# Attention scores in quarter-array products inside a fused attention + two-MLP kernel

## The chip, the cores and the metric

One core of one Trainium2 chip runs the whole program. The metric is device time in microseconds (us). The kernel before was run three times: 907.88, 909.35 and 910.19 us, median 909.35.

Engines in the views: PE is TensorE's matmuls, PEld its weight loads (each matmul has one), DVE is VectorE, ACT is ScalarE, POOL is GpSimd, SP issues the DMAs. Each engine runs its own instructions in order.

## The reference

```python
# q, k, v: (4 batches, 8 heads, 576 positions, 64)
scores = q @ k.T / sqrt(64); mask: 0 <= pos_q - pos_k < 64
attn = softmax(scores); x = (attn @ v) -> (2304 tokens, 512)
# first layer:  h = x @ w_in (512 x 2048); g = relu(h)**2; x = g @ w_out
# second layer: h = x @ w_in; g = (a0 + a1 h + a2 h^2 + a3 h^3) / (1 + |b0||h| + |b1|h^2 + 1e-6); out = g @ w_out
```

The weights arrive as float64, everything else as float32.

## The kernel before

**Blocks and layers.** The 2304 tokens are cut into five blocks: four of 512 tokens, one of 256. For each block the first layer runs 16 steps; step `j` makes 128 rows of `h` (line 516: 12 matmuls), squares them on ACT and DVE, and adds their part of the output (line 536: 12 matmuls). The second layer does the same (lines 516 and 538) after all blocks have passed the first. Each float32 operand is split in two, and three products of the parts are summed; these products are of type float32r, one instruction each.

**Weights.** `convert` turns 1/32 of a layer's weights from float64 bits into two float32r parts: a DMA into one of three `raw` buffers, ACT (329), DVE (331, 334, 337), ACT (346), DVE (347). The first layer's 32 conversions take place during block 0, step by step with their use. The second layer's 32 take place during blocks 1 to 3.

**Attention.** It is computed in 18 sub-blocks of 128 tokens, `i` = 0 to 17, each with two groups `gl` of 64 queries; a group sees 128 keys. Sub-blocks 0 to 3 come before block 0; the others go piecewise between the matmuls of the first layer, one block ahead of their use: 4 to 7 in block 0, 8 to 11 in block 1, and so on. Sub-block 17 is done in block 3. The steps of a sub-block:
- `q`, `k`: four transposes on PE (404, 420) give the queries and keys with the head dimension on the partitions, two heads in the two halves of 64 partitions. `k` is copied out by DVE or ACT. `q` is copied out by two ACT instructions (411), each taking 64 partitions to a zero-padded buffer `qT`, where each head's 64 queries stand beside 64 columns that stay zero outside that head's partitions. The factor 1/8 is applied there. `qT` has three buffers for sub-blocks 0 to 3 and one after that; they are zeroed at the start on POOL (200).
- `s` (438), two pieces, `n` = 0 and 1, of two head pairs each: four products of 128 x 128 weights (a head pair's padded queries) by 128 columns (the keys). With the padding, one product gives two heads' scores, 64 rows each. These operands are plain float32, and each product is recorded as two instructions. `top` (449) on DVE adds the mask and takes the row maximum, ACT exponentiates (454), DVE normalises (458 to 460).
- `p` (471), two pieces: transposes of the probabilities, copied out by ACT or DVE (476).
- `x` (487): 16 products of 128 x 64 weights (the values of one head) by 64 columns (probabilities). The two heads of a pair write the two halves of the output partitions, so that they use the two column halves of the array. Each is again two instructions. The output is split into `xh` (499) and `xl` (500).

**Order.** A planner (`Plan.run`) takes the items with rough costs, a due time and what they depend on. At each turn it picks the item that can start first, then the one due first. Items that name both ACT and DVE go to the one that can start sooner. The resulting order is fixed in the program; at run time each engine waits where its data is late. Before block 0 attention has eight PSUM banks to use; afterwards it has two, `t0` and `t1`, in turns.

Of the kernel before, what the change touches and what calls it, by code (L numbers as in the profile page):

```python
# [20 lines left out]
class Buf:  # L21
    """What one place (an SBUF or PSUM buffer) holds for a while; made when it is first written."""

# [23 lines left out]
class Plan:  # L47
    """Orders the program. Every engine runs its instructions in the order they are emitted in, so an
    item should come when its data is there: of what can start, what is due first goes first.
    Work is added in an order that respects the data flow; costs are rough, in nanoseconds."""  # L50

# [90 lines left out]
def window_attention__moe_relu2__moe_rational_kernel(  # L142
# [12 lines left out]
):  # L155
    """Sliding-window attention, then two dense MoE layers.

    The weights come as the raw bits of float64; float32 is put together from the two words.
    float32 products run as float32r passes: an operand x is split exactly into
    H (12 significant bits) and L = x - H (12 bits), and HH + HL + LH is summed in PSUM.  # L160
    The first layer's weights stay in SBUF while all tokens pass; the second layer's parts are
    made meanwhile, wait in DRAM, and take the first's places as its last block frees them.
    """
    nc = tc.nc
# [23 lines left out]

# [1 line left out]
    A.preload_act_table_set("natural_log_exp_and_others")  # L190
    ident = const.tile([128, 128], F32, name="ident")
    make_identity(nc, ident)
    QT = ("qT0", "qT1", "qT2")
    q_tiles = {QT[0]: const.tile([128, HP, 2, 128], F32, name="qT0")}
    x1_before = sb.tile([128, KT, 512], F32R, tag="xh1", name="xh1").bitcast(F32).rearrange(
        "p c t -> p (c t)").rearrange("p (i c g q) -> p i c g q", i=2, c=HP, g=2)
    for i in range(2):
        q_tiles[QT[1 + i]] = x1_before[:, i]
    for t in q_tiles.values():
        P.memset(t, 0.0)  # L200
    mask = const.tile([128, 2, 128], F32, name="mask")
# [19 lines left out]

# [1 line left out]
    turn = {}  # L223

    def buf(place, shape, dtype=F32, pool=sb, view=None):
        """The next of the places (one name, or several that take turns)."""
        if not isinstance(place, str):
            n = turn.get(place, 0)
            turn[place] = n + 1
            place = place[n % len(place)]  # L230

        def make():
            t = pool.tile(shape, dtype, tag=place, name=place)
            return view(t) if view else t

        return Buf(plan, place, make)
# [8 lines left out]
    LD, RAW, CV, R = ring("ld", 6), ring("raw", 3), ring("cv", 3), ring("r", 1)  # L245
    KTP, SM, PT = ring("kT", 2), ring("sm", 2), ring("pT", 2)
    G1 = tuple((f"gh{i}", f"gl{i}") for i in range(2))
    G2 = G1 + (("cv0", "cv1"),)

    def early(j, x, d):  # L250
        """A [128, 512] float32 buffer in the place of a weight that comes much later."""
        return buf(f"w{('ih', 'il', 'oh', 'ol')[x]}{j}", [128, DM], F32R,
                   view=lambda t: t.bitcast(F32).rearrange("p (a d) -> p a d", d=d))

# [1 line left out]
    MM = {n: 0.4167 * n + 3 for n in (256, 512)}  # L256
# [13 lines left out]

# [1 line left out]
    nat = {}  # L272
# [38 lines left out]

# [1 line left out]
    wt = {}  # L313
# [49 lines left out]

# [1 line left out]
    xt = {}  # L365
# [6 lines left out]
    def x_bufs(bi):  # L372
        if bi not in xt:
            xt[bi] = tuple(x_buf(p) for p in next_of(X))
        return xt[bi]

    def x_buf(p):
        b = buf(p, [128, KT, 512], F32R)
        if p == "xh1":
            for x in [plan.places[x] for x in QT[1:] if x in plan.places]:  # L380
                if not x.over:
                    b.prev.append(x)
                    x.over = True
        return b

    def q_buf(i):
        """Two heads' queries side by side, each in its own half of the partitions; the rest is zero."""
        p = next_of(QT) if i < NS0 else QT[0]
        return Buf(plan, p, lambda: q_tiles[p])

# [7 lines left out]
    def slot_q(i, due):  # L398
        src, ps = nat["q", i], ps_buf()

        def tr(_):
            s = src.t.rearrange("p h d -> p (h d)")
            for c in range(HP):
                T.transpose(ps.t[:, c, :], s[:, c * 128:(c + 1) * 128], ident)  # L404

        plan.add({"pe": 430}, tr, [src], [ps], due)
        t = qT[i] = q_buf(i)
        for p0 in (0, 64):
            o = lambda p0=p0: t.t[p0:p0 + 64, :, :, p0:p0 + 64]
            f = lambda p0=p0: ps.t[p0:p0 + 64].rearrange("p c (g q) -> p c g q", q=W)  # L410
            plan.add({"act": act(512, True)}, lambda e, o=o, f=f: A.activation(
                out=o(), in_=f(), func=ACTF.Copy, scale=scale), [ps], [t])

# [16 lines left out]

    def slot_s(i, n, due):
        ps, qt, kt = ps_buf(), qT[i], kT[i]

        def mm(_):
            for gl in range(2):
                for c in range(2):
                    hp = 2 * n + c
                    T.matmul(out=ps.t[:, gl * 2 + c, :], lhsT=qt.t[:, hp, gl, :],  # L438
                             rhs=kt.t[:, hp, gl * W:gl * W + 128], start=True, stop=True)

        plan.add({"pe": 880}, mm, [qt, kt], [ps], due)
        t = early(NF - 5 - i, n, 128) if i < NS0 else buf(SM, [128, 4, 128])
        sm[i, n] = t
        kind = [int((2 * i + gl) % GPB == 0) for gl in range(2)]
        nm, su, rs = (buf(ring(x, 4), [128, 4]) for x in ("nm", "su", "rs"))

        def top(_):
            for c in range(4):
                V.tensor_tensor_reduce(out=t.t[:, c, :], in0=ps.t[:, c, :], in1=mask[:, kind[c // 2], :], scale=-1.0,
                                       scalar=-NEG, op0=ALU.add, op1=ALU.min, accum_out=nm.t[:, c:c + 1])  # L450
# [27 lines left out]
    def slot_x(i, due):  # L478
# [4 lines left out]
        def mm(_):  # L483
            for hp in range(HP):
                for gl in range(2):
                    for e in range(2):
                        T.matmul(  # L487
                            out=ps.t[e * 64:(e + 1) * 64, hp, gl * W:(gl + 1) * W],
                            lhsT=vg[gl].t[:, 2 * hp + e, :],
                            rhs=pt[hp // 2].t[:, gl * 2 + hp % 2, e * 64:(e + 1) * 64],  # L490
                            start=True, stop=True,
                        )
# [11 lines left out]

# [1 line left out]
    acc = {}  # L506
# [152 lines left out]

# [1 line left out]
    coef_b, na_b, b1_b = (Buf(plan, x, lambda: None) for x in ("coef", "na", "b1"))  # L661

    def slots_of(first, last):
        """Attention's steps for sub-blocks first..last-1, each far enough behind what it needs."""
        o = []
        for i in range(first, last):
            o += [("s", i, 0)] + ([("x", i - 1)] if i > first else []) + [("s", i, 1)]
            o += [("q", i + 1)] if i + 1 < NSUB else []
            o += [("p", i, 0)]
            o += [("k", i + 1)] if i + 1 < NSUB else []  # L670
            o += [("p", i, 1)]
        return o + [("x", last - 1)]
# [8 lines left out]
    for i in range(NS0):  # L681
        load_qk(i)
        load_v(i)
    begin = ("k0,q0,k1,q1,s00,s01,k2,q2,s10,s11,p00,p01,k3,q3,s20,s21,x0,p10,p11,s30,s31,x1,p20,p21,k4,q4,x2,"
             "p30,p31,x3").split(",")
# [12 lines left out]
    for l in range(2):  # L698
# [4 lines left out]
        for s in range(len(steps) + 1):  # L703
# [30 lines left out]
            if l == 0 and s < len(steps):  # L734
                while slots and slots[0][1] < due_h(0, bi, j + 1):
                    x, d = slots.pop(0)
                    if x == ("s", NS0, 0):
                        load_v(NS0 + 1)
# [40 lines left out]
```

## Time and profile before

| | |
|---|---|
| three runs, median | 909.35 us |
| profiled execution: span from first to last instruction | 906.2 us |
| its own time outside the span | not listed in the profile |
| PE busy | 892.7 us, 99% (4912 matmuls) |
| DVE busy | 671.6 us, 74% |
| ACT busy | 579.8 us, 64% |
| POOL busy | 5.8 us |
| TensorE granted clock | 1.000 of full over the span |

A matmul's duration in the views is longer than its share of the engine, because matmuls overlap: what one costs is the distance between the starts of two that follow one another. An instruction that also waits for its weights is recorded from before that wait. So the cost of a group of PE instructions is read here from the distance between a large matmul just ahead and the second large matmul just behind it.

### The profile page before, as it was taken

How to read it: one execution, taken by the hardware profiler on the slowest of the kernel's cores; microseconds unless marked ns; L12 is line 12 of the kernel's file. 1: busy time of each engine (PE TensorE's matmuls, PEld its weight loads, DVE VectorE, ACT ScalarE, POOL GpSimd, SP SyncE). 2: the span in 40 equal slices, each digit the busy share in tenths (PEclk: the TensorE clock that was granted, in tenths of full speed). 3: DMA queues.
4: the chain of work that ended last, by engine and by line, in shares of the span. 5: the costliest groups of instructions: out<-in, count | busy, mean ns of one | idle time of the engine just before them, and what ended most of it. 6: DMA issues, size and time to landing. Idle time of an engine off the chain costs nothing.

```text
span 906.2 us, 13520 instructions
## 1 busy us (share of the span) xinstructions
PE 892.7 (99%) x4912; PEld 745.6 (82%) x4912; DVE 671.6 (74%) x1432; ACT 579.8 (64%) x1201; POOL 5.8 (1%) x20
## 2 busy tenths in 40 slices
PE   8899999999999999999999999999999999999998
PEld 7678888888888888888899888888888888888886
DVE  5999999788777732422131699999899999999994
ACT  7878787666576643544244766566667666887764
POOL 2000000000000000000000000000000000000000
PEclk9999999999999999999999999999999999999999
DMA  9877676888777621200069920120011002100001
GB/s 209 212 198 221 178 210 224 263 259 260 244 267 238 195 46 36 93 1 1 1 241 387 365 76 0 51 90 1 1 46 47 1 1 93 48 1 23 1 1 46
DMA packets 128450, 110.45 MB, mean 122 GB/s; under 512 B 78976, under 2 KB 97408, under 8 KB 128384
## 3 DMA queue, kind: packets, MB, share of 16 engines
q1 hardware_dynamic: 128384, 109.60, 38.7%
q8 instruction: 38, 0.62, 0.3%
q14 instruction: 28, 0.23, 0.1%
HBM read 78.65 MB, written 30.93 MB: 121 GB/s over the span
## 4 chain that ended last, share of the span: by engine, by line
PE 89%; DVE 4%; DMA 3%; ACT 2%; SPq 1%; issue 1%; ACTq 0%; DVEq 0%
PE h L516 31%; PE acc L538 22%; PE acc L536 20%; PE t L516 11%; PE t L438 2%; DMA raw<-in_moe_w_in_dram 2%; PE t L487 2%; PE t L471 1%; DMA w2h_d<-raw 1%; PE t L420 1%; SPq L277 1%; DVE cv L334 1%; DVE cv L337 1%; PE t L404 0%; DMA wih<-in_k_dram 0%
## 5 line engine op out<-in xcount | busy, mean ns | idle before, releaser
L516 PE MATMUL h<-xh,wih 128*128 128x512 f32 (+1 forms) x480 | 181.9, 379 | 0.2 <-ACT wih L346 0.2
L516 PE MATMUL h<-xh,wil 128*128 128x512 f32 (+1 forms) x480 | 177.8, 370 | 0.0
L516 PE MATMUL h<-xl,wih 128*128 128x512 f32 (+1 forms) x480 | 177.6, 370 | 0.0
L536 PE MATMUL acc<-gh,woh 128*128 128x512 f32 (+1 forms) x320 | 122.2, 382 | 0.1
L588 DVE TENSOR_TENSOR gl<-r,gh 128x512 fp32r<-128x512 f32 (+1 forms) x80 | 50.8, 635 | 94.1 <-ACT r L586 93.3
L536 PE MATMUL acc<-gl,woh 128*128 128x512 f32 (+1 forms) x320 | 118.6, 371 | 0.0
L536 PE MATMUL acc<-gh,wol 128*128 128x512 f32 (+1 forms) x320 | 118.5, 370 | 0.0
L516 PEld LDWEIGHTS h<-xh,wil 128*128 128x128 f32 x480 | 90.3, 188 | 16.8 <-DVE wil L347 0.4
L516 PEld LDWEIGHTS h<-xh,wih 128*128 128x128 f32 x480 | 90.4, 188 | 15.5 <-ACT wih L346 0.5
L516 PEld LDWEIGHTS h<-xl,wih 128*128 128x128 f32 x480 | 90.5, 189 | 15.0 <-DVE xl L500 0.4
L581 ACT ACTIVATE r<-h 128x512 f32<-128x512 f32 (+1 forms) x80 | 44.4, 555 | 90.1 <-PE h L516 88.0
L538 PE MATMUL acc<-woh,gh 128*128 128x512 f32 x178 | 70.0, 393 | 0.0
L538 PE MATMUL acc<-wol,gh 128*128 128x512 f32 x178 | 69.9, 393 | 0.0
L538 PE MATMUL acc<-woh,gl 128*128 128x512 f32 x178 | 69.7, 391 | 0.0
L630 DVE SCALAR_TENSOR_TENSOR kT<-kT,b,sm 128x512 f32<-128x512 f32 (+1 forms) x80 | 55.8, 697 | 18.5 <-ACT kT L625 16.7
L536 PEld LDWEIGHTS acc<-gh,wol 128*128 128x128 f32 x320 | 60.3, 188 | 10.8
L536 PEld LDWEIGHTS acc<-gh,woh 128*128 128x128 f32 x320 | 60.3, 189 | 9.9 <-DVE xl L603 0.5
L536 PEld LDWEIGHTS acc<-gl,woh 128*128 128x128 f32 x320 | 60.4, 189 | 9.5 <-DVE gl L588 0.5
L632 ACT ACTIVATE raw<-kT,cb 128x512 f32<-128x512 f32 (+1 forms) x80 | 54.8, 685 | 8.7 <-DVE kT L630 6.1
L329 ACT ACTIVATE cv<-raw 128x512 f32<-128x512 f32 x64 | 42.8, 671 | 26.2 <-DMA raw<-in_moe_w_in_dram 12.1
L516 PE MATMUL t<-xh,wih 128*128 128x512 f32 (+1 forms) x160 | 59.2, 370 | 0.0
L516 PE MATMUL t<-xl,wih 128*128 128x512 f32 (+1 forms) x160 | 59.2, 370 | 0.0
(178 smaller groups left out, 1783.6 us busy)
## 6 DMA issues: line engine op xcount, KB each, us to landing
raw<-in_moe_w_in_dram SPq DMA_DIRECT2D x32, 512.0 KB, 4.4
raw<-in_moe_w_out_dram SPq DMA_DIRECT2D x32, 512.0 KB, 4.5
w2h_d<-raw SPq DMA_DIRECT2D x32, 256.0 KB, 2.4
w2l_d<-cv SPq DMA_DIRECT2D x32, 256.0 KB, 3.4
ld<-in_v_dram SPq DMA_DIRECT2D x25, 256.0 KB, 3.5
out_dram<-ld SPq DMA_DIRECT2D x18, 256.0 KB, 2.2
x2h_d<-xh SPq DMA_DIRECT2D x4, 1024.0 KB, 4.5
x2l_d<-xl SPq DMA_DIRECT2D x4, 1024.0 KB, 6.2
```

Source lines behind the costliest of these rows:

```text
L277: nc.sync.dma_start(out=o, in_=i)
L329: plan.add({"act": act(DM)}, lambda e: A.activation(out=t.t, in_=raw.t.bitcast(F32)[:, :, 1], func=ACTF.Copy, scale=2.0 ** -112), [raw], [t])
L334: plan.add({"dve": dve(DM)}, lambda e: V.scalar_tensor_tensor(out=u(t), in0=u(t), scalar=3, in1=raw.t[:, :, 1], op0=ALU.logical_shift_left ...
L438: T.matmul(out=ps.t[:, gl * 2 + c, :], lhsT=qt.t[:, hp, gl, :], rhs=kt.t[:, hp, gl * W:gl * W + 128], start=True, stop=True)
L487: T.matmul(out=ps.t[e * 64:(e + 1) * 64, hp, gl * W:(gl + 1) * W], lhsT=vg[gl].t[:, 2 * hp + e, :], rhs=pt[hp // 2].t[:, gl * 2 + hp % 2, ...
L516: T.matmul(out=hp.t[:, :n], lhsT=w.t[:, c * 128:(c + 1) * 128], rhs=x.t[:, c, :n], start=(c == 0 and z == 0), stop=(c == KT - 1 and z == 2))
L536: T.matmul(out=acc[l, bi, m].t[:, :n], lhsT=w.t[:, ms], rhs=y.t[:, :n], start=st, stop=en)
L538: T.matmul(out=acc[l, bi, m].t, lhsT=y.t[:, ms], rhs=w.t, start=st, stop=en)
L581: plan.add({"act": act(n, True)}, lambda e: A.activation(out=r.t[:, :n], in_=hp.t[:, :n], func=ACTF.Relu), [hp], [r])
L588: plan.add({"dve": dve(n)}, lambda e: V.tensor_tensor(out=gl.t[:, :n], in0=r.t[:, :n], in1=gh.t[:, :n].bitcast(F32), op=ALU.subtract), [r, ...
L630: plan.add({"dve": dve(n, ptr=1)}, lambda e: V.scalar_tensor_tensor(out=f(h2), in0=f(h2), scalar=b1, in1=f(ab), op0=ALU.mult, op1=ALU.add) ...
L632: plan.add({"act": act(n, ptr=1)}, lambda e: A.activation(out=f(y), in_=f(h2), func=ACTF.Ln, scale=2.0 ** -63, bias=cb[:, 0:1]), [h2], [y])
```

## The change

Queries are no longer padded: `qT` is a plain [128, 4, 128] copy in one of two buffers, made by one instruction of 128 partitions on ACT or DVE. The zeroing at the start is gone. `s` is one piece per sub-block: 16 products of 64 x 64 weights by 128 columns. Head `e` of a pair uses the row half `e` of the array; query group `gl` goes to the column half `e ^ gl`, and to its own PSUM bank `ps[gl]`. The factor 1/8 moves into `top`. Softmax tiles are now one per query group instead of one per two head pairs, and `x` picks its probabilities accordingly. In the planner `s` counts as 900 instead of 2 x 880.

```diff
-    QT = ("qT0", "qT1", "qT2")
-    q_tiles = {QT[0]: const.tile([128, HP, 2, 128], F32, name="qT0")}
...
-    for t in q_tiles.values():
-        P.memset(t, 0.0)
...
-        t = qT[i] = q_buf(i)
-        for p0 in (0, 64):
-            o = lambda p0=p0: t.t[p0:p0 + 64, :, :, p0:p0 + 64]
-            f = lambda p0=p0: ps.t[p0:p0 + 64].rearrange("p c (g q) -> p c g q", q=W)
-            plan.add({"act": act(512, True)}, lambda e, o=o, f=f: A.activation(
-                out=o(), in_=f(), func=ACTF.Copy, scale=scale), [ps], [t])
+        t = qT[i] = buf(QTP, [128, HP, 128])
+        plan.add({"act": act(512, True), "dve": dve(512)}, lambda e: (
+            A.copy(out=t.t, in_=ps.t) if e == "act" else V.tensor_copy(t.t, ps.t)), [ps], [t])
...
-    def slot_s(i, n, due):
-        ps, qt, kt = ps_buf(), qT[i], kT[i]
+    def slot_s(i, due):
+        ps, qt, kt = [ps_buf() for _ in range(2)], qT[i], kT[i]
         def mm(_):
-            for gl in range(2):
-                for c in range(2):
-                    hp = 2 * n + c
-                    T.matmul(out=ps.t[:, gl * 2 + c, :], lhsT=qt.t[:, hp, gl, :],
-                             rhs=kt.t[:, hp, gl * W:gl * W + 128], start=True, stop=True)
-        plan.add({"pe": 880}, mm, [qt, kt], [ps], due)
+            for hp in range(HP):
+                for gl in range(2):
+                    for e in range(2):
+                        r = slice(e * 64, e * 64 + 64)
+                        o = (e ^ gl) * 64
+                        T.matmul(out=ps[gl].t[o:o + 64, hp, :], lhsT=qt.t[r, hp, gl * W:(gl + 1) * W],
+                                 rhs=kt.t[r, hp, gl * W:gl * W + 128], start=True, stop=True)
+        plan.add({"pe": 900}, mm, [qt, kt], ps, due)
+        for gl in range(2):
+            softmax(i, gl, ps[gl])
...
-                V.tensor_tensor_reduce(..., in1=mask[:, kind[c // 2], :], scale=-1.0,
+                V.tensor_tensor_reduce(..., in1=mask[:, kind, :], scale=-scale,
...
-                            rhs=pt[hp // 2].t[:, gl * 2 + hp % 2, e * 64:(e + 1) * 64],
+                            rhs=pt[gl].t[:, hp, (e ^ gl) * 64:((e ^ gl) + 1) * 64],
...
-            o += [("s", i, 0)] + ([("x", i - 1)] if i > first else []) + [("s", i, 1)]
+            o += [("s", i)] + ([("x", i - 1)] if i > first else [])
```

## Rows read from the trace of the kernel before

**Rows 1.** Stages: length, busy us (instructions) of PE, PEld, DVE, ACT, POOL; clock, DMA share, GB/s.
```profile
0.00:35.00 35.00, 27.35 (x294) 24.48 (x295) 25.05 (x110) 26.93 (x88) 5.83 (x20) 1.00 0.91 202
35.00:62.00 27.00, 25.04 (x150) 19.89 (x148) 26.38 (x72) 20.19 (x54) 0.00 (x0) 1.00 0.92 226
62.00:146.00 84.00, 83.77 (x490) 68.92 (x489) 79.00 (x187) 66.80 (x144) 0.00 (x0) 1.00 0.66 197
146.00:422.00 276.00, 275.88 (x1590) 228.02 (x1589) 165.87 (x435) 159.15 (x376) 0.00 (x0) 1.00 0.53 167
```

**Rows 2.** What PE waited for from 62 to 422 us: total, times, longest.
```profile
PE h L516 <- ACT wih L346: 0.2, 1, 0.2
```

**Rows 3.** Stages again: from the first scores to the last conversion of the first layer.
```profile
9.00:138.00 129.00, 121.71 (x854) 100.64 (x854) 122.77 (x349) 105.84 (x272) 0.00 (x0) 1.00 0.78 207
```

**Rows 4.** DVE and PE timelines: block 0's last `w_in` conversion and its use (start, duration).
```profile
134.87 0.69 DVE L347 TENSOR_TENSOR wil<-cv,wih 128x512 fp32r<-128x512 f32 x1
...
136.67 0.40 PE L516 MATMUL h<-xh,wih 128*128 128x512 f32 x1
```

**Rows 5.** DMA issues held back, 0 to 146 us: for what; total, times, longest.
```profile
SPq L277 <- DVE cv L337: 32.7, 17, 3.6
```

**Rows 6.** The chain of waits: twelve large matmuls in one piece.
```profile
90.47 2.72 PE h L516 x12
```

**Rows 7.** PE timeline around one score piece.
```profile
105.42 0.39 PE L516 MATMUL h<-xh,wil 128*128 128x512 f32 x1
105.65 1.05 PE L438 MATMUL t<-kT,qT 128*128 128x128 f32 x8
106.46 0.48 PE L536 MATMUL acc<-gh,woh 128*128 128x512 f32 x1
106.77 0.40 PE L536 MATMUL acc<-gl,woh 128*128 128x512 f32 x1
```

**Rows 8.** PE timeline around one attention-output step.
```profile
109.05 0.39 PE L536 MATMUL acc<-gh,wol 128*128 128x512 f32 x1
109.37 1.15 PE L487 MATMUL t<-pT,ld 128*64 128x64 f32 x32
110.45 0.50 PE L516 MATMUL h<-xh,wih 128*128 128x512 f32 x1
110.79 0.39 PE L516 MATMUL h<-xl,wih 128*128 128x512 f32 x1
```

**Rows 9.** PE timeline inside the first attention-output step: third and last of eight entries.
```profile
18.79 0.29 PE L487 MATMUL t<-woh,woh 128*64 128x64 f32 x4
...
19.38 0.29 PE L487 MATMUL t<-wol,wol 128*64 128x64 f32 x4
```

**Rows 10.** PE and PEld timelines cut off at 109.46, just after Rows 8's step began.
```profile
109.37 0.28 PE L487 MATMUL t<-pT,ld 128*64 128x64 f32 x2
...
109.37 0.20 PEld L487 LDWEIGHTS t<-pT,ld 128*64 128x64 f32 x4 [0.35 <-ACT wih L346]
```

**Rows 11.** Timelines of ACT, PE and DVE at the first scores.
```profile
6.54 1.21 ACT L411 ACTIVATE qT<-h 64x512 f32<-64x512 f32 x2
...
7.84 2.02 PE L438 MATMUL acc<-kT,qT 128*128 128x128 f32 x16 [1.10 <-issue]
...
9.13 0.29 DVE L449 CUSTOM_DVE_ANT_0 wih<-acc,mask 128x128 f32<-128x128 f32 x1 [2.17 <-PE acc L438]
```

**Rows 12.** The copies of `q` on ACT (min/median/max ns), of `k` on ACT and DVE (busy, mean ns).
```profile
L411 ACT ACTIVATE qT<-t x26: 571/592/597, 41.6 to 375.6; 64x512 f32<-64x512 f32 x26
...
L428 ACT COPY kT<-t 128x512 f32<-128x512 f32 x13 | 7.6, 584 | 14.2 <-PE t L420 10.1 <-DVE kT L425 4.0
...
L429 DVE COPY kT<-t 128x512 f32<-128x512 f32 x3 | 2.1, 687 | 3.4 <-PE t L420 3.4
```

**Rows 13.** POOL timeline: the last of the zeroing, and the last mask step.
```profile
2.13 1.85 POOL L200 MEMSET xh<- 128x1024 f32 x2
...
5.87 0.55 POOL L210 TENSOR_SCALAR_AFFINE_SELECT mask<-mask 64x128 f32<-64x128 f32 x2
```

More of the change, by code (lines that the diff above doesn't have):

```diff
@@ L192, in window_attention__moe_relu2__moe_rational_kernel @@
     make_identity(nc, ident)
-    QT = ("qT0", "qT1", "qT2")
-    q_tiles = {QT[0]: const.tile([128, HP, 2, 128], F32, name="qT0")}
[L195 to L198, printed above, removed]
-    for t in q_tiles.values():
-        P.memset(t, 0.0)
     mask = const.tile([128, 2, 128], F32, name="mask")
@@ L245, in window_attention__moe_relu2__moe_rational_kernel @@
     LD, RAW, CV, R = ring("ld", 6), ring("raw", 3), ring("cv", 3), ring("r", 1)
-    KTP, SM, PT = ring("kT", 2), ring("sm", 2), ring("pT", 2)
+    KTP, QTP, SM, PT = ring("kT", 2), ring("qT", 2), ring("sm", 2), ring("pT", 2)
     G1 = tuple((f"gh{i}", f"gl{i}") for i in range(2))
@@ L373, in x_bufs @@
         if bi not in xt:
-            xt[bi] = tuple(x_buf(p) for p in next_of(X))
+            xt[bi] = tuple(buf(p, [128, KT, 512], F32R) for p in next_of(X))
         return xt[bi]
[L377 to L389, printed above, removed]
     ps_places = [ALL_PS]
@@ L429, in slot_k, with softmax @@
             V.tensor_copy(t.t[:, :, W:W + 128], ps.t)), [ps], [t])
-    def slot_s(i, n, due):
-        ps, qt, kt = ps_buf(), qT[i], kT[i]
+    def slot_s(i, due):
+        ps, qt, kt = [ps_buf() for _ in range(2)], qT[i], kT[i]
         def mm(_):
-            for gl in range(2):
-                for c in range(2):
-                    hp = 2 * n + c
-                    T.matmul(out=ps.t[:, gl * 2 + c, :], lhsT=qt.t[:, hp, gl, :],
-                             rhs=kt.t[:, hp, gl * W:gl * W + 128], start=True, stop=True)
-        plan.add({"pe": 880}, mm, [qt, kt], [ps], due)
-        t = early(NF - 5 - i, n, 128) if i < NS0 else buf(SM, [128, 4, 128])
-        sm[i, n] = t
-        kind = [int((2 * i + gl) % GPB == 0) for gl in range(2)]
+            for hp in range(HP):
[8 more added lines that the diff above has]
+            softmax(i, gl, ps[gl])
+    def softmax(i, gl, ps):
+        t = early(NF - 5 - i, gl, 128) if i < NS0 else buf(SM, [128, 4, 128])
+        sm[i, gl] = t
+        kind = int((2 * i + gl) % GPB == 0)
         nm, su, rs = (buf(ring(x, 4), [128, 4]) for x in ("nm", "su", "rs"))
@@ L448, in top @@
             for c in range(4):
-                V.tensor_tensor_reduce(out=t.t[:, c, :], in0=ps.t[:, c, :], in1=mask[:, kind[c // 2], :], scale=-1.0,
+                V.tensor_tensor_reduce(out=t.t[:, c, :], in0=ps.t[:, c, :], in1=mask[:, kind, :], scale=-scale,
                                        scalar=-NEG, op0=ALU.add, op1=ALU.min, accum_out=nm.t[:, c:c + 1])
@@ L683, in window_attention__moe_relu2__moe_rational_kernel @@
         load_v(i)
-    begin = ("k0,q0,k1,q1,s00,s01,k2,q2,s10,s11,p00,p01,k3,q3,s20,s21,x0,p10,p11,s30,s31,x1,p20,p21,k4,q4,x2,"
+    begin = ("k0,q0,k1,q1,s0,k2,q2,s1,p00,p01,k3,q3,s2,x0,p10,p11,s3,x1,p20,p21,k4,q4,x2,"
              "p30,p31,x3").split(",")
@@ L736, in window_attention__moe_relu2__moe_rational_kernel @@
                     x, d = slots.pop(0)
-                    if x == ("s", NS0, 0):
+                    if x == ("s", NS0):
                         load_v(NS0 + 1)
```

## The prediction

> **What bounds the kernel now.** I read four views, in this order. The engine table by stage comes first, to see who is full where [rows 1]. From 62 us on PE is busy for the whole of both stages shown (83.77 of 84 us, then 275.88 of 276), at full granted clock. Before that it is not: 7.65 of the first 35 us are idle. The list of waits says the same more sharply: from 62 to 422 us, the stretch that holds nearly all the inserted attention, PE waited 0.2 us in total [rows 2]. A microsecond taken off PE there is a microsecond off the end, unless something else takes over.
>
> The something else differs by block. Up to the end of block 0 the weight conversions run just ahead of their use: between 9 and 138 us DVE is busy 122.8 of 129 us, 95% [rows 3]; the last `w_in` conversion ends at 135.56 and PE begins with those weights at 136.67, 1.1 us later [rows 4]. DMA does not lead there: its issues wait 32.7 us in all for DVE to release a buffer [rows 5]. So in block 0 a faster PE gains little more than DVE lets it. From 146 to 422 us DVE has 166 of 276 us and ACT 159 [rows 1]: there PE alone sets the pace. Sub-blocks 8 to 17, ten of the eighteen, are computed there, but for the very first piece.
>
> **The change part by part.**
>
> **The score products.** Twelve large matmuls follow one another in 2.72 us, 0.227 each [rows 6]. From the large matmul ahead of a score piece (105.42) to the second one behind it (106.77) is 1.35 us; two large ones are 0.45, so the piece costs 0.90 us, 0.112 for each of its 8 records [rows 7]. Two pieces make 1.79 us per sub-block.
>
> The new step has 16 products, two records each: 32, of the same 128 columns. Each uses a quarter of the array. If all four quarters work at once, that is 8 rounds of 0.112, 0.90 us. The trace before has no product on a row half, so this must be bounded. The nearest row is the `x` step, on column halves. There a head pair's two products for one query group are 4 records; from the entry at 18.79 to that at 19.38 are five entries, 0.118 us each, 0.059 per product [rows 9]. A product of two records with 128 columns takes 0.224; one with 64 would take 0.112 alone. So 0.059 is two at a time: the column halves do overlap. Fully overlapped quarters give 0.90 us; quarters of which only two work at a time give 16 rounds, 1.79 us; none at all, 3.6 us, which the column rows exclude for this half of the matter.
>
> **Order of issue.** The two records of a product stand one behind the other on the same quarter. If a start had to keep that order, the second would hold back the next quarter's first, and never more than two quarters would work. The trace cut off 0.09 us after an `x` step began shows two matmuls started together and already four weight loads, and the next matmuls not yet [rows 10]: the second column half did not wait for the first's second record. That is why I take 0.90, not 1.79.
>
> The Trainium skill says otherwise ("TensorE: Matmul & The Clock Gate", Part 3, The mechanism): matmuls start and end strictly in program order, only weight loads overtake. By it the step would be 16 rounds, rival A's price below. These rows speak against it for column halves.
>
> **What surrounds the step.** A step on parts of the array does not join smoothly to full-array matmuls. The `x` step from 109.05 to 110.79 is 1.74 us; less two large matmuls 1.28; its 32 records at 0.118 per four are 0.94 [rows 8, 9]. The rest, 0.34 us, is entering and leaving; the weight loads, otherwise ahead of the matmuls, stop for 0.35 us just before the step [rows 10]. The score pieces before have nothing of it: 0.90 is 8 even records. The new step gets it once. Ends: nothing (0.90 in all) and twice as much; I take the `x` step's 0.34: 0.90 + 0.34 = 1.24 us. Saving 1.79 - 1.24 = 0.55, rounded down to 0.54 us per sub-block; in sub-blocks 8 to 17, 5.4 us.
>
> **Head and block 0.** The first scores wait for two ACT copies, 1.21 us [rows 11]; one of about 0.58 (the full-width `k` copy) replaces them [rows 12], so they start 0.6 us earlier. The first `top` now needs the whole step, 1.24 instead of 0.90 us, less a saving on PE that nobody waits for: 0.3 back, 0.3 to 0.4 us earlier. I take 0.4.
>
> ACT loses an instruction of 0.6 us per sub-block, 4.8 us for sub-blocks 0 to 7, on an engine with 105.8 of 129 us busy [rows 3, 12]. DVE, which is fuller, gains only if the planner hands ACT more of the copies that either may do (0.69 us on DVE, 0.58 on ACT). Ends: all of the freed time used so, 4.8/0.58 = 8 copies, 5.5 us off DVE, of which the two engines balanced would keep half, 2.8; the other way, some `q` copies land on DVE, two of them 1.4 us lost. I take 1.2 us earlier. It fits the cover: PE's own share of block 0, 3.5 sub-blocks at 0.54, gives 1.9, so PE can follow conversions that end 1.6 us earlier. If they do not, 1.1 us [rows 4] is all that PE can gain in block 0.
>
> **At nothing.** The zeroing on POOL ends at 3.98 us and the masks at 6.42, while the first user of a mask comes at 9.13 [rows 11, 13]: hidden by the first loads and transposes. The factor 1/8 in `top` changes a constant of an instruction. `top`, exponentials, `p` and `x` keep count and shape. The second `qT` buffer lets a `q` copy go ahead of the previous scores; PE does not wait for it now [rows 2].
>
> **An added wait.** `s` needs both `t0` and `t1` free at once; before, each piece needed one. Queued behind it on PE are the large matmuls of the layer. I price it at nothing because the same two banks already alternate through `q`, `k`, `p` and `x` with 0.2 us of waits [rows 2]; the other end is in rival B.
>
> **Sum.** 5.4 + 0.4 + 1.2 = 7.0 us. The profiled span of 906.2 becomes 899.2. The profile does not list what lies around the span; the median of the runs is 3.15 above it, and nothing there changes: 909.35 - 7.0 = 902.35, so 902.3 us.
>
> **Rivals.**
>
> **A: the row halves take turns (the change doesn't do what it says).** No row shows two row halves at work together. Then the step is 16 rounds, 1.79 + 0.34 = 2.13 us, 0.34 more than before. It decides once a sub-block's scores cost more than about 1.9 us (1.79 plus the tenth of the 1.6 us won in the head). Ten sub-blocks: +3.4; in block 0 PE is then the later one, 3.5 x 0.34 = 1.2 more; the head gives back 0.4 to 0.6. About +4.0: 913.3 us. For it: only column halves are shown. Against it: the overlap in [rows 10] looks like each part of the array having its own progress.
>
> The Trainium skill has a rule that would bring A about ("TensorEngine Tiling (Array Packing)", Gotcha 1: PSUM Pressure): row tiles can't access the same PSUM bank at the same time. Here both heads of a query group write one bank from different row halves, though on different partitions. The Trainium skill's page "PSUM — Partial Sum Buffer", section "PSUM bank collisions raise a hardware error", narrows it to the same bank and the same 32 partitions, which this layout never has. No run here shows either.
>
> **B: PE waits for the pair of banks.** In block 0 DVE runs at 95% [rows 3]; if the reader of one bank is one DVE instruction (0.69 us) late at `s`, PE stands, and the matmuls behind it. In all 14 inserted sub-blocks that is 9.7 us, more than the gain; in half of them 4.8: 902.3 + 4.8 = 907.1. For it: the pair is held by two row maxima in a row. Against it: [rows 2].
>
> **How the numbers follow.** A difference below about 0.3%, 2.7 us, can't be told from none. Forecast 0.74; its own range is 898.8 (no entering cost: 0.90 us a step, 8.9 + 1.6 = 10.5 off) to 905.5 (twice the entering cost, 2.0, and the head gaining little), of which 0.70 is faster by over 0.3% and 0.04 within. A 0.14: slower 0.12, within 0.02. B 0.12: faster 0.03, within 0.07, slower 0.02. Sum: faster 0.73, same 0.13, slower 0.14. The range goes from 898.5 to 911.0, which takes in B and the mild part of A and leaves out some 0.14.
>
> **What would show it.** Right: 576 records of 64 x 64 weights in the score line, in groups of 32; measured as above, such a group costs 1.2 to 1.3 us, and four matmuls start close together about every 0.11 us. The line of the `q` copy has 18 instructions of 128 partitions. The first layer's blocks 1 to 3 get shorter by some 2.2, 2.2 and 1.1 us, the second layer stays. Wrong: a group at 2.1 us (A); PE idle just ahead of the score or `x` groups with DVE as releaser (B); the last `w_in` conversion of block 0 no earlier than 135.5 (then the head gave nothing, and about 903.5 follows).

## The result and the profile after

The changed kernel takes 900.37 us (median of four runs, 899.32 to 901.27), beside 909.32 us for the kernel before on the same chip: ratio 0.9908, 95% interval 0.9894 to 0.9921, or 9.0 us less by the medians (7.2 to 9.6 by the interval). The forecast was 902.3 us, faster, in a range of 898.5 to 911.0.

The two profiled executions stand closer together: spans of 899.4 and 906.2 us, 6.8 apart; 7.0 had been forecast. The rest of the 9.0 is where these executions lie among their runs. The one of after took 901.19 us, 0.8 above its median and 1.8 above its span. With the same 1.8 around it, the one of before took some 908.0, 1.3 below its median. The forecast had put 3.15 us around the span.

The stages of the changed kernel (columns as in [rows 1]), then the stretch of [rows 3]:

```profile
0.00:35.00 35.00, 26.51 (x382) 21.89 (x383) 25.48 (x118) 24.93 (x88) 3.13 (x17) 0.95 0.94 204
35.00:62.00 27.00, 25.39 (x175) 19.67 (x174) 26.69 (x76) 24.34 (x66) 0.00 (x0) 1.00 0.93 235
62.00:146.00 84.00, 81.76 (x515) 64.94 (x517) 76.25 (x170) 59.30 (x126) 0.00 (x0) 0.98 0.65 191
146.00:415.00 269.00, 269.00 (x1741) 217.63 (x1730) 165.01 (x439) 156.09 (x373) 0.00 (x0) 1.00 0.56 173
...
9.00:138.00 129.00, 119.20 (x952) 94.09 (x951) 120.02 (x341) 101.14 (x267) 0.00 (x0) 0.97 0.78 206
```

After block 0 PE is full, as before. In block 0 it is not: 81.76 of 84 us, where [rows 1] had 83.77. What PE waited for from 28 to 146 us (total, times, longest):

```profile
PE h L499 <- ACT wih L338: 1.6, 2, 1.4
PE h L499 <- DVE wil L339: 1.2, 3, 0.8
PE h L499 <- ACT xh L482: 0.6, 1, 0.6
PE t L417 <- ACT kT L403: 0.5, 1, 0.5
...
```

The first two lines are converted weights that came late; 2.0 us of them lie after 62 us, where [rows 2] had 0.2 for the same cause. No line names a bank that scores waited for.

PE around one score step, to be read as [rows 7 and 8]:

```profile
164.59 0.39 PE L499 MATMUL h<-xh,wil 128*128 128x512 f32 x1
164.91 1.10 PE L417 MATMUL t<-kT,qT 64*64 64x128 f32 x32
165.95 0.50 PE L499 MATMUL h<-xh,wih 128*128 128x512 f32 x1
166.29 0.40 PE L499 MATMUL h<-xl,wih 128*128 128x512 f32 x1
```

From 164.59 to 166.29 is 1.70 us; less two large matmuls 1.24 us. The median of all steps that stand between large matmuls is 1.235, where before's two pieces took 1.782. The same view cut off at 165.00 and at 165.10 counts what has started:

```profile
164.91 0.34 PE L417 MATMUL t<-kT,qT 64*64 64x128 f32 x4
164.91 0.45 PE L417 MATMUL t<-kT,qT 64*64 64x128 f32 x8
```

Four records start at once, then four more: four quarters, none of which waits for another's second record.

Where the blocks of the first layer begin, read from the first large matmul of each (us):

| | before | after | difference so far |
|---|---|---|---|
| block 0 | 35.2 | 33.1 | -2.1 |
| block 1 | 142.2 | 143.2 | +1.0 |
| block 2 | 250.0 | 248.8 | -1.2 |
| block 3 | 358.2 | 354.4 | -3.8 |
| block 4 | 455.5 | 450.2 | -5.3 |
| second layer | 501.2 | 495.9 | -5.3 |
| end of span | 906.2 | 899.4 | -6.8 |

So the start gave 2.1 us, block 0 lost 3.1, blocks 1 to 3 gave 6.2, and the second layer, which has no attention in it, gave 1.5. The amount of work ahead of each of these starts is the same in both kernels (372 large matmuls and eight sub-blocks' scores ahead of block 1), so they can be compared.

### The profile page after: what moved, and what is told of

Read it like the earlier page. It is cut to its first block, busy times and chain, and to the rows that moved or that the text cites. A ratio compares the mean times of both kernels' runs of the same rounds, so it can differ in the third digit from the quotient of the medians.

```text
span 899.4 us, 14102 instructions
## 1 busy us (share of the span) xinstructions
PE 883.6 (98%) x5200; PEld 729.9 (81%) x5200; DVE 667.7 (74%) x1428; ACT 570.4 (63%) x1187; POOL 3.1 (0%) x17
## 4 chain that ended last, share of the span: by engine, by line
PE 90%; DVE 6%; DMA 2%; ACT 1%; issue 1%; POOL 0%; POOLq 0%; ACTq 0%; DVEq 0%
PE h L499 31%; PE acc L521 22%; PE acc L519 20%; PE t L499 11%; PE t L470 2%; DMA raw<-in_moe_w_in_dram 1%; PE t L417 1%; PE t L454 1%; DVE cv L329 1%; DVE cv L326 1%; PE t L382 1%; PE t L395 1%; DVE raw L323 1%; DMA raw<-in_moe_w_out_dram 1%; DVE sm L432 0%
## 5 line engine op out<-in xcount | busy, mean ns | idle before, releaser
L571 DVE TENSOR_TENSOR gl<-r,gh 128x512 fp32r<-128x512 f32 (+1 forms) x80 | 50.9, 636 | 105.4 <-ACT r L569 105.1
L499 PE MATMUL t<-xh,wil 128*128 128x512 f32 (+1 forms) x160 | 59.2, 370 | 0.0
```

The costliest lines, as they stand in the source:

```text
L499: T.matmul(out=hp.t[:, :n], lhsT=w.t[:, c * 128:(c + 1) * 128], rhs=x.t[:, c, :n], start=(c == 0 and z == 0), stop=(c == KT - 1 and z == 2))
L571: plan.add({"dve": dve(n)}, lambda e: V.tensor_tensor(out=gl.t[:, :n], in0=r.t[:, :n], in1=gh.t[:, :n].bitcast(F32), op=ALU.subtract), [r, ...
```

## The experiments

"Block 0's end" is the first large matmul of block 1 in the profile. Ratios are to the kernel before, on the same chip.

**e7: the quarters by themselves.** At the start, 16 records on one quarter, then on two in each of the three ways, then on four, then 32 on four; between them full products. Only the time within the inserted piece is read. Each triple below is where a product goes: first row (0 or 64), first column, PSUM bank.

```diff
+        part(8, [(0, 0, 0)])
...
+        part(8, [(0, 0, 0), (0, 64, 1)])
...
+        part(8, [(0, 0, 0), (64, 0, 1)])
...
+        part(8, [(0, 0, 0), (64, 64, 0)])
...
+        part(8, [(0, 0, 0), (64, 64, 0), (0, 64, 1), (64, 0, 1)])
...
+        part(16, [(0, 0, 0), (64, 64, 0), (0, 64, 1), (64, 0, 1)])
```

> The changed kernel with a longer warm-up on PE, to time the quarters by themselves: runs of 8 products of 64x64 weights by 128 columns (16 records), between pairs of full-array products: on one quarter; on two column halves; on two row halves of one column half with two banks; on the two diagonal quarters writing one bank on different partitions; on all four; and 16 products on all four. The total time is not of interest (some 5 to 10 us more). Theory (each quarter proceeds by itself): 1.79, 0.90, 0.90, 0.90, 0.45 and 0.90 us, each plus the same entering and leaving. Rival A of the prediction (row halves take turns): 1.79 for the two row halves and for the diagonal, 0.90 for four. A rule that one bank is not written by two row halves at once: 1.79 for the diagonal only.

PE's timeline, each piece and the full products behind it:

```profile
8.55 1.96 PE L667 MATMUL acc<-ident 64*64 64x128 f32 x16
10.44 0.71 PE L662 MATMUL acc<-ident 128*128 128x128 f32 x4
11.08 1.09 PE L667 MATMUL acc<-ident 64*64 64x128 f32 x16
12.10 0.71 PE L662 MATMUL acc<-ident 128*128 128x128 f32 x4
12.74 1.09 PE L667 MATMUL acc<-ident 64*64 64x128 f32 x16
13.76 0.71 PE L662 MATMUL acc<-ident 128*128 128x128 f32 x4
14.40 1.09 PE L667 MATMUL acc<-ident 64*64 64x128 f32 x16
15.42 0.71 PE L662 MATMUL acc<-ident 128*128 128x128 f32 x4
16.07 0.67 PE L667 MATMUL acc<-ident 64*64 64x128 f32 x16
16.66 0.71 PE L662 MATMUL acc<-ident 128*128 128x128 f32 x4
17.30 1.10 PE L667 MATMUL acc<-ident 64*64 64x128 f32 x32
18.34 0.71 PE L662 MATMUL acc<-ident 128*128 128x128 f32 x4
```

From the start of each piece to that of the full products behind it: 1.89 us on one quarter; 1.02 on two column halves, on two row halves, and on the diagonal, whose two quarters write one bank on different partitions; 0.59 on four. Rival A is refuted for row halves in one bank too. Twice the records on four take 1.04, so 16 more cost 0.45, 0.112 for each round of four. The 1.04 is also what the score step takes in the kernel from its start to the next (164.91 to 165.95). One bank on the same partitions was not tried.

**e2: two quarters of four.** Both query groups of a head go to the same column half; `x` picks its probabilities accordingly.

```diff
-                        o = (e ^ gl) * 64
+                        o = e * 64
```

> The changed kernel with the scores on two quarters only: head 0 always in row half 0 and column half 0, head 1 in row half 1 and column half 1; x reads its probabilities accordingly. Nothing else differs. This takes the fourfold overlap away and leaves the rest of the change. A step should be 16 rounds of 0.112 plus 0.34, 2.13 us, 0.89 more. Theory (PE sets the pace only from block 1 on; block 0 is set by the conversions): ten sub-blocks, +8.9 us: about 909.3, as slow as before the change. Rival (PE sets the pace in block 0 too): fourteen sub-blocks, +12.5: about 912.9. If instead the gain came mainly from the copies and the zeroing: about 900 to 903.

Measured 910.03 us (909.08 to 913.15, ten runs), ratio 1.0015 (1.0004 to 1.0026), 9.7 above the changed kernel: the theory's 8.9 more than the rival's 12.5. One step:

```profile
165.76 0.39 PE L499 MATMUL h<-xh,wil 128*128 128x512 f32 x1
166.08 1.96 PE L417 MATMUL t<-kT,qT 64*64 64x128 f32 x32
167.97 0.50 PE L499 MATMUL h<-xh,wih 128*128 128x512 f32 x1
168.31 0.40 PE L499 MATMUL h<-xl,wih 128*128 128x512 f32 x1
```

From 165.76 to 168.31 less two large matmuls, the step costs 2.09 us, and blocks 1 to 3 take 315.5 instead of 307.0: 8.5, for ten steps of 0.86 more. So without the second pair of quarters the whole gain is gone, and rival A's 2.13 us is about what two at a time would have cost.

**e1: the same 16 products, one quarter after the other.**

```diff
-            for hp in range(HP):
-                for gl in range(2):
-                    for e in range(2):
+            for gl in range(2):
+                for e in range(2):
+                    for hp in range(HP):
```

> The changed kernel with one edit: the score products are issued quarter by quarter, all four head pairs of one quarter behind one another (8 records on the same quarter), instead of going round the four quarters. Theory 1 (each quarter has a queue of its own, deep enough): the order doesn't matter, a step stays at 1.24 us and the time at about 900.4. Theory 2 (starts keep the program's order): only where one quarter's run ends and the next begins do two overlap; a step takes about 29 to 32 rounds of 0.112 plus 0.34, 3.6 to 3.9 us, 2.4 to 2.7 more in each of the ten sub-blocks that PE paces: about 925 to 937. Theory 3 (own queues, but only a few records deep): in between, by the step's length in the trace.

918.41 us (917.73 to 918.93), ratio 1.0106 (1.0091 to 1.0121), and 2.69 us a step (168.61 to 171.76 less two large matmuls); blocks 1 to 3 take 321.5 us, 14.5 more than with the changed kernel. This is the third expectation. PE's timeline cut off at 169.40, at 169.45 and at 169.90:

```profile
168.93 0.65 PE L417 MATMUL t<-kT,qT 64*64 64x128 f32 x4
168.93 0.81 PE L417 MATMUL t<-kT,qT 64*64 64x128 f32 x6
168.93 1.14 PE L417 MATMUL t<-kT,qT 64*64 64x128 f32 x12
```

Four records start alone. With the fifth of the first quarter (169.41) the first of the second starts (169.42), though three of the first quarter's eight are still to come; from there they run in pairs, and the third quarter joins at 169.91. The fourth quarter joins at 170.4, again with the fifth record of the one before it. So the quarters neither take strict turns nor are free of each other: in this run an instruction gets past three that wait for another quarter, no more. Going round the quarters is worth 1.46 us a step.

**e3: the queries copied by two ScalarE instructions,** as before the change, without the padding.

```diff
-        plan.add({"act": act(512, True), "dve": dve(512)}, lambda e: (
-            A.copy(out=t.t, in_=ps.t) if e == "act" else V.tensor_copy(t.t, ps.t)), [ps], [t])
+        for p0 in (0, 64):
+            plan.add({"act": act(512, True)}, lambda e, p0=p0: A.copy(
+                out=t.t[p0:p0 + 64], in_=ps.t[p0:p0 + 64]), [ps], [t])
```

> The changed kernel with the query copy made as before the change: two ACT instructions of 64 partitions each instead of one on ACT or DVE (the buffers stay unpadded, the zeroing stays away). It undoes the relief of ACT alone. Theory (block 0 ends no earlier in the changed kernel, so the relief is worth nothing): within 1 us of 900.4. Rival (the prediction's: 0.4 us at the first scores and 1.2 us in block 0): about 902.

903.47 us (902.88 to 904.45), ratio 0.9942 (0.9928 to 0.9956): 3.1 slower than the changed kernel, more than the theory allowed and nearer to the rival. Block 0 begins at 36.7 (33.1 with one copy) and ends at 144.9 (143.2). The single copy, which may also go to VectorE (3 of 18 do), is worth some 3 us; 1.7 of it is there at the end of block 0. This does not add up with e2: the second pair of quarters (9.7 us) and the single copy (3.1) together are worth more than the whole gain of 9.0, which suggests that the rest of the change costs something. It shows in block 0: with two copies, as the kernel before has them, block 0 ends at 144.9, 2.6 later than there (142.2). No run takes this rest by itself.

**e4 and e5: conversions made lighter,** in the kernel before (e4) and in the changed one (e5). The first two VectorE instructions of each conversion of the first layer are left out.

```diff
+        if l:
             plan.add({"dve": dve(DM, True)}, lambda e: V.tensor_scalar(...bitwise_and), ...)
             plan.add({"dve": dve(DM)}, lambda e: V.scalar_tensor_tensor(...bitwise_or), ...)
```

> The kernel before, with a lighter conversion of the first layer's weights: two of the four DVE instructions of each conversion (the sign mask and the first merge) are left out for layer 0, so its weights are not the reference's. It frees DVE of about 0.94 us in each of 32 conversions of block 0. To be read beside the changed kernel with the same cut. By itself: DVE no longer paces block 0; both theories expect a few us off, 903 to 907.

> The changed kernel with the same two DVE instructions left out of layer 0's conversions. Theory (block 0 hides the change's gain because the conversions pace it): without them the change gains in block 0 too, 3.5 sub-blocks at 0.55 us and the head's 1.6, so the distance to the lighter kernel before grows from 9.0 to about 11 to 12.5 us. Rival (block 0's lack of gain comes from PE itself, its fallen clock and the order of the steps): the distance stays at 8 to 9.5.

e4: 909.73 us (907.45 to 912.27, ten runs), ratio 1.0007 (0.9993 to 1.0021), where 903 to 907 was expected. e5: 896.10 us (895.39 to 896.58), ratio 0.9854 (0.9839 to 0.9868). The same lighter conversion gives nothing before the change and 4.3 us after it; the two kernels are 13.6 us apart, a little beyond the theory's 11 to 12.5. The engines in e5's block 0, columns as above:

```profile
62.00:146.00 84.00, 84.00 (x552) 67.73 (x551) 66.31 (x156) 62.51 (x145) 0.00 (x0) 1.00 0.80 242
```

PE is full, and block 0 ends at 137.5 instead of 143.2. So conversions hold the changed kernel's block 0 back, though e5 makes VectorE's load lighter and each conversion shorter at once and so does not tell which counts. e4 says less: its PE waited 3.6 us for loads of `q`, and its granted clock fell to half for 3.4 us at 96.3, which may have eaten a gain. That PE, not the conversions, was full before is read from [rows 1 and 2].

**e6: the planner told 1240 for the step** instead of 900, its measured cost.

> The changed kernel with the planner's price of the score step set to what it measured, 1240 instead of 900 ns. Only the order of instructions can change. Theory (blocks 1 to 3 are paced by PE whatever the order, and block 0 by the conversions): within 1 us of 900.4. Rival (a step planned too short puts PE's next items ahead of their data, which costs the waits seen in block 0): 1 to 2.5 us faster, 898 to 899.4.

900.64 us (899.56 to 902.59), ratio 0.9900 (0.9884 to 0.9917): the same as the changed kernel, as the theory had it.

**e9: sub-blocks 0 to 3 on two quarters.** In the changed profile the granted clock falls to half, the 1.2 GHz level, twice, for 3.4 us from 25.1 and from 90.0 us. The stretch with the second fall (columns as in [rows 1], the clock is the third number from the end), and PE's timeline there:

```profile
89.00:94.00 5.00, 4.76 (x15) 3.54 (x16) 4.93 (x12) 3.34 (x6) 0.00 (x0) 0.66 0.34 111
...
87.06 0.39 PE L519 MATMUL acc<-gh,wol 128*128 128x512 f32 x1
88.88 0.49 PE L499 MATMUL h<-xh,wih 128*128 128x512 f32 x1 [1.43 <-ACT wih L338]
...
90.34 0.63 PE L499 MATMUL h<-xh,wih 128*128 128x512 f32 x1
90.77 0.63 PE L499 MATMUL h<-xl,wih 128*128 128x512 f32 x1
```

PE had idled 1.43 us for weights until 88.88; the clock fell 1.1 us later, and large matmuls start 0.43 apart instead of 0.23. An idle stretch of that length does not always bring a fall: in e3 PE idled 2.25 us before 42.4 and 1.51 before 50.9, at full clock from 30.7 on. e9 asked whether the fall at the start, where the shorter scores leave PE idle, costs time; `x` picks its probabilities accordingly.

```diff
-                        o = (e ^ gl) * 64
+                        o = (e ^ gl if i >= NS0 else e) * 64
```

> The changed kernel, with the scores of sub-blocks 0 to 3 (before block 0) on two quarters only and all others on four. PE then works 0.86 us longer in each of four steps in which it otherwise waits. Theory (the shorter steps leave PE idle at the start, and the granted clock falls to half for 3.4 us there, which the profiles with the longer steps don't show): the clock stays at 1.0 and the time falls by 0.5 to 1.7 us, to about 899. Rival (the start is paced by ACT and DVE, and longer steps only delay them): 0 to 2 us slower than 900.4.

901.31 us (900.55 to 901.73), ratio 0.9911 (0.9896 to 0.9926). Its profiled clock is full in all stages, and the time is no better, in the rival's range: block 0 begins at 35.0 instead of 33.1. So nothing is won by avoiding the fall in this way. What the fall alone costs is not shown, because e9 takes it away and adds some 3.4 us of PE work in one edit.

**e10: the last subtraction of a conversion on GpSimd or VectorE,** as the planner likes, to relieve VectorE in block 0.

```diff
-    ENGINES = ("pe", "act", "dve", "dma")
+    ENGINES = ("pe", "act", "dve", "dma", "pool")
...
-        plan.add({"dve": dve(DM)}, lambda e: V.tensor_tensor(
+        plan.add({"dve": dve(DM), "pool": 1300} if l == 0 else {"dve": dve(DM)}, lambda e: (P if e == "pool" else V).tensor_tensor(
```

> The changed kernel, all of its work done, with the last step of layer 0's conversions (the subtraction that makes the low part) allowed on POOL as well as on DVE; the planner takes whichever can start sooner, with a guessed 1300 ns for POOL. Theory (conversions pace block 0 of the changed kernel, DVE above all, and POOL is idle): DVE loses up to 19 us of 125, the conversions end earlier and PE becomes the pace again: up to the 4.3 us that the lighter conversions gave, 896 to 899. Rival (a conversion's own length or POOL's speed matters more than DVE's load): no gain, 900 to 903.

915.28 us (914.04 to 917.57), ratio 1.0066 (1.0053 to 1.0080), 15 slower than the changed kernel, with block 0's end at 155.9. The theory is refuted, and the rival, which had no gain but 900 to 903 us, had the direction only. GpSimd took 26 subtractions, 1.41 and 1.71 us long in the mean of its two lines, and this is what they did to VectorE:

```profile
97.25 1.77 POOL L339 TENSOR_TENSOR wol<-cv,woh 128x512 fp32r<-128x512 f32 x1 [1.28 <-ACT woh L338]
...
97.79 1.78 DVE L326 SCALAR_TENSOR_TENSOR cv<-cv,raw 128x512 uint32<-128x512 uint32 x1
99.49 0.68 DVE L483 TENSOR_TENSOR xl<-t,xh 128x512 fp32r<-128x512 f32 x1
100.09 0.68 DVE L329 SCALAR_TENSOR_TENSOR cv<-raw,cv 128x512 uint32<-128x512 uint32 x1
```

VectorE's merge, 0.69 us otherwise, takes 1.78 beside GpSimd's subtraction, and the next merge, alone, 0.68. The Trainium skill states it ("SBUF — State Buffer", Who interferes with whom): a VectorE instruction with two inputs in SBUF contends with a GpSimd instruction that reads SBUF. These rows agree.

**e11: the tiles moved,** by 2560 bytes, with one x tile placed first (the kernel before placed it first too); no instruction of the steady part differs.

```diff
+    pad = const.tile([128, 640], F32, name="pad")
+    P.memset(pad[:, 0:1], 0.0)
...
+    x1_first = sb.tile([128, KT, 512], F32R, tag="xh1", name="xh1").bitcast(F32)
+    P.memset(x1_first[:, 0, 0:1], 0.0)
```

> The changed kernel with its SBUF buffers at other addresses: a 2560-byte pad ahead of everything, and the place of xh1 taken first, as in the kernel before. No instruction of the stages differs. It asks where 2 us of the gain came from that the score steps don't explain: in the kernels with the old layout the second layer takes 450.6 us (two profiles), in those with the new one 449.0 to 449.2 (seven profiles). Theory (placement of the buffers): the second layer moves away from 449.1, to 450 or more, and the time to 901 to 903. Rival (something in the order of the instructions): it stays at 449.1 and the time at 900.4.

901.10 us (900.25 to 901.83), ratio 0.9905 (0.9889 to 0.9921). One line of the second layer's products in the kernel before, after and in e11 (min/median/max ns, start of the first and of the last):

```profile
L538 PE MATMUL acc<-woh,gh x178: 387/393/400, 515.1 to 901.8; 128*128 128x512 f32 x178
```

```profile
L521 PE MATMUL acc<-woh,gh x178: 387/389/400, 509.8 to 895.1; 128*128 128x512 f32 x178
```

```profile
L525 PE MATMUL acc<-woh,gh x178: 387/393/402, 509.1 to 895.6; 128*128 128x512 f32 x178
```

From first to last: 386.7, 385.3 and 386.5 us. With the tiles moved, the changed kernel's second layer takes its old time again, 1.2 us more. The whole second layer takes 405.0 us before, 403.5 after and 404.8 in e11. So most of that part of the gain is where tiles lie, not the score layout; which tile does it was not tried. The order of the program moves it too: in e6, where only the planner's price differs, it is 402.8. The whole times don't tell e11 from the changed kernel, since its block 0 ends at 142.3 instead of 143.2.

**e12 and e13: VectorE relieved in block 0.** e12 sends block 0's second squares to ScalarE; e13 also the last multiplication of the softmax of sub-blocks 4 to 7.

Of the edits below, the first is in both, the second in e13 alone.

```diff
-        plan.add({"act": act(n), "dve": dve(n)}, lambda e: (
+        plan.add({"act": act(n)} if bi == 0 else {"act": act(n), "dve": dve(n)}, lambda e: (
...
+            for c in range(4):
+                A.activation(out=t.t[:, c, :], in_=t.t[:, c, :], func=ACTF.Abs, scale=rs.t[:, c:c + 1])
```

> The changed kernel, except that in block 0 of the first layer all second squares go to ScalarE (five that the plan gave to VectorE, 3.5 us of VectorE's time, become 3.2 us of ScalarE's); nothing is left out. Theory (block 0 of the changed kernel goes at the pace of the conversions, and of their engines VectorE, 76 of 84 us busy, is the late one): with 3.5 us less on it block 0 ends 2 to 3.5 us earlier and the kernel takes 897 to 898.5 us. Rival (the pace is set by the round trip between ScalarE and VectorE or by the loads, not by VectorE's time; ScalarE's longer queue then costs as much): 900 to 903 us.

> As e12, and the last multiplication of the softmax of sub-blocks 4 to 7 goes to ScalarE too, as four instructions of 128 columns for each group: VectorE loses 5.5 us more (eight groups of 0.69), ScalarE gains some 9 us. Theory (VectorE's time sets block 0): up to the 4.6 us that the conversions hide are given back, 895.5 to 897.5 us, no further, since TensorE is full from there. Rival (round trip or loads set it): ScalarE's longer path to the second block's probabilities makes it slower than e12, 900 to 905 us.

e12: 898.42 us (897.93 to 898.93), ratio 0.9894 (0.9879 to 0.9909), with block 0's end at 139.8, 3.4 us earlier (2.5 against e9 and e11, whose clock did not fall in block 0). That is in the theory's favour, and it is the fastest kernel of the study with the whole computation; but its interval overlaps the changed kernel's, so a gain over that is likely and not shown. e13: 899.92 us (898.23 to 901.70), ratio 0.9910 (0.9893 to 0.9926): no further gain, and short of the theory's 895.5 to 897.5. Its block 0 is not earlier either: the last product of block 0's output begins at 147.9 us, in e12 at 146.4. In block 2 its PE waits 1.8 us in three places, in e12 never, and block 4 begins at 450.8, 447.0 in e12. What brings these waits was not looked into further, so that VectorE's time alone sets block 0 is not shown.

## Why the prediction was right, and where it was not

**The score products: right.** 1.24 us was forecast and 1.24 is measured: 8 rounds of 0.112 (e7) and about 0.34 for entering and leaving. Ten steps of 0.547 are 5.5 us (forecast 5.4); blocks 1 to 3 got shorter by 2.2, 2.6 and 1.5 us (forecast 2.2, 2.2, 1.1). Of the difference some 0.5 us is again the spacing of the large matmuls, 0.2300 us instead of 0.2304 in the mean of these blocks, and not the scores.

**Order of issue: right, for a narrower reason.** The step taken from [rows 10], that a second record does not hold back the next quarter, holds for this order of the loops. e1 shows that it holds only while few records of one quarter stand in a row: two in the changed kernel, eight in e1. It also shows that PE does not start its instructions strictly in the program's order, as "The chip, the cores and the metric" says of every engine. By the strict order of starts that the Trainium skill gives ("TensorE: Matmul & The Clock Gate", Part 3, The mechanism) the step would have been 2.13 us; the four starts at once behind one another (4 records by 165.00, 8 by 165.10) and e1's first two quarters disagree with it. The Trainium skill's rule on row halves and one bank ("TensorEngine Tiling (Array Packing)", Gotcha 1) did not bite on different partitions (e7: 1.02 us for the diagonal, as for the others).

**Head and block 0: the step that failed.** It was to bring 0.4 and 1.2 us; in the profile block 0 ended 1.0 us later. The head did its part, and more: scores start at 7.02 instead of 7.84 [rows 11], the first `top` at 8.28 instead of 9.13, block 0 at 33.1 instead of 35.2. ACT and DVE were relieved too: 101.1 and 120.0 busy us between 9 and 138, against 105.8 and 122.8 [rows 3]. But the last `w_in` conversion ended at 136.27, not 135.56 [rows 4]. That was the sign named for a head that gives nothing and a time of about 903.5; the sign came, although the head had given, and the total made up for it elsewhere.

The relief of ACT was worth about what was forecast for head and block 0, 1.6 us: without it (e3) block 0 ends 1.7 us later. What failed is the step from that relief to an earlier end of the conversions: the rest of the change was put at nothing there, and e3 beside the kernel before has it at 2.6 us later. What in the rest costs this was not taken apart. PE's own share was also counted too high: three score steps lie in block 0, sub-blocks 5 to 7, not 3.5. The line of DVE's first step of a conversion, 62 to 142 us, in the kernel before and after (busy, mean ns, idle time ahead of it):

```profile
L331 DVE TENSOR_SCALAR raw<-raw 128x512 uint32<-128x512 uint32 x25 | 10.5, 423 | 1.9 <-ACT cv L329 1.9
```

```profile
L323 DVE TENSOR_SCALAR raw<-raw 128x512 uint32<-128x512 uint32 x24 | 10.2, 427 | 5.6 <-ACT cv L321 5.5
```

What DVE gained in time it stood waiting for ACT's step ahead of it. That step waits for the weights' loads. In all its waits are no longer than before (9.0 and 9.2 us between 62 and 142), but for `w_in` they come in longer pieces (total, times, longest; before, then after):

```profile
ACT cv L329 <- DMA raw<-in_moe_w_in_dram: 4.2, 4, 1.4
```

```profile
ACT cv L321 <- DMA raw<-in_moe_w_in_dram: 6.7, 5, 3.3
```

The longest one, in the changed kernel's chain of waits:

```profile
78.14 6.18 DMA raw<-in_moe_w_in_dram
...
84.41 0.67 ACT cv L321
...
85.10 0.43 DVE raw L323
...
89.85 1.98 PE h L499 x4
```

DVE's last merge releases the buffer at 78.1, the load takes 6.18 us, and behind it stand DVE's longest wait (2.4 us, until 85.10) and PE's 1.43 us before 88.88. In the chain from 60 to 146 us such loads have 18.7%, in the kernel before 5.2%. So "DMA does not lead there" was read too quickly from [rows 5]: that an issue waits for DVE does not take the load's own time out of the round from buffer to buffer.

And PE, which had been the full engine of block 0, went ahead of the conversions and waited for weights. So here the score step's saving was hidden: 4.3 us come out when conversions are lighter (e5), and the block's end moves by 3.4 when VectorE is relieved (e12). Part of the +1.0 may be the clock's fall at 90 us: without one in block 0, e11, which has the changed kernel's instructions, ended it at 142.3, and e9 at 142.4. (e6, also without, ended it at 144.8, but has one more score step ahead of that.) The other three runs of the changed kernel have a mean granted clock of 0.998, the profiled one 0.996, which fits one fall and two; so an end near 142.3 may be the common case. Even that is no gain where 1.6 us was forecast. Which part of the round is late, VectorE's time, its queue's order, the loads or the number of buffers, stays open: no run changes one of them alone.

**At nothing, and the added wait: right.** No score step waited for the pair of banks, so rival B is out; POOL's zeroing, 2.7 of its 5.8 us, is gone, and nothing in the trace had waited for it. The planner's price made no difference (e6). What was wrong at nothing, the rest of the change in block 0, stands above.

**The sum was right by misses that cancel, which is luck.** Against the forecast of -7.0, the profiles have -6.8: block 0's end was 2.6 us worse than forecast (+1.0 for -1.6), blocks 1 to 3 0.8 better, and the second layer, forecast to stay, 1.5 better, most of which e11 gives to where the tiles lie. The last 2 us between 902.3 and 900.37 are the 3.15 us that were put around the span, where the runs list 1.8, and the place of the profiled execution 0.8 above its median.

## What to carry to other kernels

Small products gain from quarters of the array only if the order of issue goes round them: here the same 16 products cost 1.24 us going round and 2.69 one quarter after the other. A saving on the engine that is full counts until another falls behind it, so name stage by stage what is late next; freed busy time on an engine that stands in a long chain is not yet an earlier end, so look at what else is in that round, the loads too. And a forecast that hits can do so by misses that cancel: check it against the starts of the stages, not against the total.

## What the runs showed of the hardware that was not expected

- Two quarters on the diagonal, in one bank on different partitions, run as well together as any two: 1.02 us for 16 records, 1.89 on one quarter.
- In e1 an instruction for a free quarter passes three that wait for a busy one, no more: each next quarter starts with the fifth of the eight records of the one before.
- A GpSimd subtraction of 1.77 us stretches a VectorE merge beside it from 0.69 to 1.78 us (e10).
- In the changed kernel the granted clock fell to half for 3.4 us in the middle of block 0, 1.1 us after PE had idled 1.43 us, with matmuls 0.43 us apart instead of 0.23; e3's PE idled 2.25 us without a fall.
- The same large matmuls stand 0.3% closer together or further apart by where tiles lie: 385.3 or 386.5 us from first to last for one line of the second layer's (e11).
